# Feed-forward phase of a fused forward and backward pass: operands turned on TensorE ahead of their group, turned stores in SP's queue, half chunks in pairs

## The chip, the core and the metric

The kernel runs on one core of a Trainium2 chip. Its time is device microseconds, the median of a few runs. The core has a matrix engine (PE, with PEld for its weight loads), three engines for elementwise work (DVE, ACT, POOL) and SP, which here only issues DMAs. POOL issues DMAs too. The two issuers have a queue each, and 16 DMA engines serve both.

## The reference

A transformer layer with recurrent memory attention and a gated feed-forward network (FFN), and the gradients of all its inputs, in bf16:

```
h  = x + A(layernorm(x), mem0, Wq, Wk, Wv, Wo)    # segments of 32 rows, one after the other
h2 = h + (silu(hn @ w_gate) * (hn @ w_up)) @ w_down, hn = layernorm(h)
_out, _vjp = jax.vjp(_f, A_x, A_mem0, A_Wq, A_Wk, A_Wv, A_Wo, B_w_gate, B_w_up, B_w_down)
_grads = _vjp(grad_out)
```

x has 2048 rows of 448, the FFN is 1792 wide, and the attention has 16 heads of 256 and 8 rows of memory. The memory that leaves one segment enters the next, so attention runs through 64 segments in order, and its backward pass through the same 64 in reverse.

## The kernel before

Four stages follow each other on PE. `forward_chain` runs the 64 segments. `ffn_phase` does the FFN forward and backward for 8 **groups** of 256 rows (G = 2 tiles of 128). `backward_chain` runs the 64 segments backward; it is a Python generator, and its first loads are written into the program from within the FFN's last group by calls of `back()`, one step up to each `yield`. `tail_phase` forms the weight gradients from what the other stages stored to DRAM.

The order on each engine comes from a scheduler at build time: it takes ready instructions by priority, which falls with their place in the program. `tc.issue_after(ins)` puts an instruction behind another one on its engine. On the chip each engine, and SP's and POOL's queue of DMAs, then works strictly in that order: an instruction that waits holds all behind it.

SBUF is cut by hand. `W`, `A` and `B` are three arenas (arW, arA, arB in the profile), and `A(35, ...)` is a view that starts at KB 35 of each partition. Buffers of different stages lie over each other, so many waits are for a place to become free.

One group (lines 874 to 971; n counts the groups in order, gi is the group's place in the rows):

- `load_in` (L279) fetches the rows of h and of grad_out through SP. DVE normalises h into `hn` (L887). Both are 448 wide and padded to 512, so that they make KC = 4 chunks of 128 columns; the fourth is half zeros, and so are the weights' last 64 rows (memsets at L826 to L832).
- hn and grad_out are turned into `hnT` and `doT`: groups 0 and 1 by PE (L893) with a copy out of PSUM by DVE or ACT (L894), groups 2 to 7 by DMA transposes in SP's queue (L896).
- `proj` (L856) multiplies weights by a turned operand: 7 PSUM banks, in each 2 column blocks by 4 chunks, 56 matmuls of 128x256 (L862). It runs three times: gate (ACT sigmoid L904, DVE product L905), up (ACT copy L908, DVE product z L909), and dz from `doT` (ACT copy L912). PSUM has 5 banks for this.
- DVE forms the derivative of silu in three passes of 128x3584 (L914, L921, L922), and from it and dz the gradients u and g (L941 to L943).
- PE multiplies z by w_down (28 matmuls, L934), and u and g by the turned weights (56 matmuls, L958). `ln_bwd` (L252 to L263) ends the tile on DVE.
- `tmajor` (L850) turns z, u and g with DMA transposes in SP's queue (L853) into three staging buffers in turn, and POOL stores those (L854). The last group is turned by PE (`tmajor_pe`).

Around the phase: the forward pass leaves four blocks of 512 KB whose turned copies go out through two staging buffers in arA (transposes L554 in SP's queue, stores L511 `X_o` in POOL's). Group 1 writes its gate into the same places. At the other end the steps of `back()` load, in this order: q, k and three quarters of Wk turned (L1044); Wo turned (L1046); Wv turned (L1050); `vT`, the values of the last segment (L1011), which lies over the last group's dz; and, behind the FFN, the first quarter of Wk (L1054) and Wq (L1055).

Of the kernel before, what the change touches and what calls it, by code (L numbers as in the profile page):

```python
# [15 lines left out]
P = 128  # L16
# [249 lines left out]
class _FFNLoads:  # L266
# [19 lines left out]
    def rows(self, dst, src):  # L286
        k, sync = self.k, self.k.nc.sync
        sync.dma_start(out=dst[:, 0:3, :], in_=src[0:3 * P, :].rearrange("(kc p) n -> p kc n", p=P))
        return sync.dma_start(out=dst[0:64, 3, :], in_=src[3 * P:k.D, :])

    def turned_rows(self, dst, src):
        sync = self.k.nc.sync
        sync.dma_start(out=dst[:, 0:3, :], in_=src[:, 0:3, :])
        return sync.dma_start(out=dst[0:64, 3, :], in_=src[0:64, 3, :])
# [17 lines left out]
class _TailLoads:  # L312

    def __init__(self, k):
        W, A, NT, NB = k.W, k.A, k.NT, k.NB
        self.k = k
        self.first = [W(17.5 + 4 * i, 2048) for i in range(3)] + [A(4 * i, 2048) for i in range(4)]
        self.slots = [A(48 + 4 * i, 2048) for i in range(3)] + [W(60, 2048), W(92, 2048)] + [W(96 + 4 * i, 2048) for i in range(7)] \
            + [W(32 + 4 * i, 2048) for i in range(7)] + [W(64 + 4 * i, 2048) for i in range(7)] + [A(17.5 + 4 * i, 2048) for i in range(4)] + self.first[0:3]
# [474 lines left out]
def ffn_phase(k: _K, back):  # L794
# [24 lines left out]
    dz_b = [W(54.5, G, FC, P), A(49, G, FC, P)]  # L819
    tstg_b = [W(92, FC, P), W(120.5, FC, P), B(5, FC, P)]  # L820
# [4 lines left out]
    for i in range(4):  # L825
        nc.gpsimd.memset(hn_b[i][:, D:DP], 0.0)  # L826
        nc.gpsimd.memset(dout_b[i][:, D:DP], 0.0)
    for i in range(2):
        nc.gpsimd.memset(dhb_b[i][:, D:DP], 0.0)
    nc.gpsimd.memset(Wg_sb[64:P, 3, :], 0.0)  # L830
    nc.gpsimd.memset(Wu_sb[64:P, 3, :], 0.0)
    nc.gpsimd.memset(WdT_sb[64:P, 3, :], 0.0)  # L832

# [15 lines left out]

    def tmajor(src, t, tt, dst):  # L850
        stg = tstg_b[rot[0] % 3]
        rot[0] += 1
        nc.sync.dma_start_transpose(out=stg, in_=src[:, tt].rearrange("p f n -> p (f n)"))  # L853
        nc.gpsimd.dma_start(out=dst[t * P:(t + 1) * P, :], in_=stg.rearrange("p f n -> p (f n)"))  # L854

    def proj(Wt, xT, fn):  # L856
        for fp in range(FC // 2):
            ps = k.ps1()
            for f2 in range(2):
                c = 2 * fp + f2  # L860
                for kc in range(KC):
                    nc.tensor.matmul(ps[:, f2 * 256:(f2 + 1) * 256], lhsT=Wt[:, kc, c * P:(c + 1) * P], rhs=xT[:, kc, :],  # L862
                                     start=(kc == 0), stop=(kc == KC - 1))
            fn(ps[:].rearrange("p (f t n) -> p t f n", f=2, t=G), slice(2 * fp, 2 * fp + 2))
# [9 lines left out]
    for n, gi in enumerate(list(range(last - 1)) + [last, last - 1]):  # L874
        hnT, doT = hnT_b[n % 2], doT_b[n % 2] if n < last else doT_last
        t1 = t1_b[n == last]
        if n > 1:
            load_in(n, gi)
        if n == last - 3:
            rstd(NT - 4, NT)  # L880
        for tt in range(G):
            t = G * gi + tt
            i = 2 * (n % 2) + tt
            rows = slice(t * P, (t + 1) * P)
            h_t, hn_t, dout_t = h_b[i], hn_b[i], dout_b[i]
            with tc.issue_after(k.last_x["v"].ins):
                nc.vector.tensor_scalar(out=hn_t[:, 0:D], in0=h_t, scalar1=mv2[:, t, 0:1], scalar2=rstd2[:, t:t + 1],  # L887
                                        op0=ALU.subtract, op1=ALU.mult)
            for src, dst in ((hn_t, hnT), (dout_t, doT)):
                if n < 2:  # L890
                    pt = k.ps1()[:].bitcast(BF16)
                    for kc in range(KC):
                        nc.tensor.transpose(pt[:, kc * P:(kc + 1) * P], src[:, kc * P:(kc + 1) * P], k.ident[:, :])  # L893
                    k.evac(dst[:, :, tt * P:(tt + 1) * P], pt[:, 0:DP].rearrange("p (c n) -> p c n", n=P))  # L894
                else:
                    nc.sync.dma_start_transpose(out=dst[:, :, tt * P:(tt + 1) * P], in_=src)  # L896
            nc.gpsimd.dma_start(out=dr["HN"][rows, :], in_=hn_t[:, 0:D])
        if n == last:
            back()
        e = n % 2  # L900
        g, z, dz, u, sg = g_b[e], z_b[e], dz_b[e], u_b[e], sg_b[e]
# [12 lines left out]
        to_v = nc.vector.tensor_tensor(out=t1, in0=g, in1=sg, op=ALU.mult)  # L914
# [6 lines left out]
        nc.vector.tensor_tensor(out=t1, in0=g, in1=t1, op=ALU.subtract)  # L921
        nc.vector.tensor_tensor(out=sg, in0=t1, in1=sg, op=ALU.add)  # L922
        proj(Wu_sb, hnT, up)
# [16 lines left out]
        for tt in range(G):  # L940
            nc.vector.tensor_tensor(out=u[:, tt], in0=dz[:, tt], in1=u[:, tt], op=ALU.mult)  # L941
            nc.vector.tensor_tensor(out=u[:, tt], in0=u[:, tt], in1=sg[:, tt], op=ALU.mult)
            nc.vector.tensor_tensor(out=g[:, tt], in0=dz[:, tt], in1=g[:, tt], op=ALU.mult)  # L943
        if n == last:
            back()
            for tt in range(G):
                tmajor_pe(z, G * gi + tt, tt, dr["Zt"], (W(120.5, F), B(5, F))[tt])
        for tt in range(G):
# [13 lines left out]
            ln_bwd(k, [(dh_t, dout_b[2 * e + tt][:, 0:D], 0, D)], pdh[:, 0:D], hn_b[2 * e + tt][:, 0:D], rstd2[:, t:t + 1], t1f[:], junk)  # L962
# [3 lines left out]
            nc.gpsimd.dma_start(out=dr["DHb"][rows, :], in_=dh_b)  # L966
        if n == last:
            for tt in range(G):
                t = G * gi + tt
                tmajor_pe(u, t, tt, dr["DGP"], A(7 * tt, F))  # L970
                tmajor_pe(g, t, tt, dr["DU"], A(7 * tt + 3.5, F))


def backward_chain(k: _K):
# [16 lines left out]
    vT = A(48, 16, 2 * L)  # L991
# [4 lines left out]
    dh_h = [B(9.875, 448).bitcast(FP32), A(50.5, 448).bitcast(FP32)]  # L996
# [452 lines left out]
```

## Time and profile before

| | us |
|---|---|
| median of 5 runs | 3155.65 (3151.09 to 3157.26) |
| the profiled execution: its time | 3155.65 |
| the profiled execution: its span, first to last instruction | 3153.8 |
| forward segments, up to the first matmul of L862 | 1060.8 |
| FFN, from there to the first L1093 of the backward pass | 332.4 |
| backward segments, from there to the first L1329 of the tail | 1091.8 |
| tail | 668.7 |

The profiled execution took as long as the median run, and 1.85 us lie outside its span. The stages are read from PE's timeline by the line numbers. Over the whole span PE is busy for 92%, DVE for 43%, ACT for 34% and POOL for 21%.

The timeline prints start, duration, engine, line, operation, output<-inputs and the count of merged instructions; in brackets the engine's idle time before and what ended it. The waits view prints who waited for whom, with us in total, times, and the longest.

### The profile page before, as it was taken

Reading aid. Unit: us, or ns where it says so; the run is one execution under the profiler, and the core shown is the slowest. Engines: PE = TensorE matmul, PEld = TensorE weight load, DVE = VectorE, ACT = ScalarE, POOL = GpSimd, SP = SyncE. Lnnn points to the kernel's source line nnn. Section 1 sums busy time; section 2 is a strip of 40 time slices with the busy share of each in tenths; the row PEclk is TensorE's granted clock in tenths of the full one; section 3 lists DMA queues with packets and bytes.
Section 4 is the critical chain, followed back from the end, with each engine's and each line's share of the span. In section 5 each row is a group of like instructions: output and inputs, shape, how many; then the busy total and the mean of one; then the engine's idle time right before and its main releaser. Section 6 shows DMA issues by size and latency. Waiting matters only on the chain. (4 is left out here: it accounts for less than half of the span.)

```text
span 3153.8 us, 108004 instructions
## 1 busy us (share of the span) xinstructions
PE 2911.4 (92%) x47486; PEld 1759.2 (56%) x47486; DVE 1370.2 (43%) x3437; ACT 1060.4 (34%) x2505; POOL 667.1 (21%) x1540
## 2 busy tenths in 40 slices
PE   5999999999988869979999999999999799999998
PEld 3555555455544556656666666666666454444443
DVE  4555555455555567764445444454444201111110
ACT  2444444344444323333344333343334101111210
POOL 2222222222222221121112111121211111211111
PEclk9999999999999989999999999999999999999999
DMA  6667766766755998894545545546544899969941
GB/s 238 166 176 173 175 170 169 179 165 168 194 162 165 260 224 196 204 322 116 139 133 145 135 132 140 133 130 153 136 134 137 259 283 248 198 179 188 200 148 64
DMA packets 758075, 554.79 MB, mean 176 GB/s; under 512 B 621924, under 2 KB 656596, under 8 KB 755172
## 3 DMA queue, kind: packets, MB, share of 16 engines
q1 hardware_dynamic: 702436, 372.51, 49.8%
q0 software_dynamic: 55168, 175.36, 16.5%
q8 instruction: 373, 6.11, 0.8%
q14 instruction: 98, 0.80, 0.1%
HBM read 167.32 MB, written 234.23 MB: 127 GB/s over the span
## 5 line engine op out<-in xcount | busy, mean ns | idle before, releaser
L75 DVE CAST arA<-psf 128x256 bf16<-128x256 f32 (+3 forms) x933 | 426.9, 480 | 788.3 <-PE psf L1308 258.9
L76 ACT CAST arA<-psf 128x96 bf16<-128x96 f32 (+5 forms) x915 | 352.4, 409 | 1047.3 <-PE psf L1308 256.5
L1142 PE MATMUL po<-arW,arA 128*32 128x448 bf16 x6144 | 348.3, 357 | 6.7 <-DMA arW<-Tk 6.7
L1308 PE MATMUL psf<-arW,arA 128*128 128x512 bf16 x960 | 241.9, 379 | 0.0
L1093 PEld LDWEIGHTS <-arW 128*128 128x128 bf16 x8192 | 213.4, 96 | 28.2 <-issue 28.1
L1308 PEld LDWEIGHTS <-arA 128*128 128x128 bf16 x1440 | 136.0, 98 | 165.1 <-issue 13.7
L1093 PE MATMUL psf<-arA,arW 128*128 128x40 bf16 x8192 | 217.2, 180 | 8.8 <-DVE arA L1168 5.1
L644 PE MATMUL psf<-arW,arA 128*64 128x512 bf16 x1536 | 220.3, 388 | 0.0
L1142 PEld LDWEIGHTS <-arA 128*32 128x32 bf16 x6144 | 152.9, 97 | 118.3 <-issue 9.6
L533 PE MATMUL psf<-arW,arA 128*32 128x512 bf16 x3072 | 193.6, 385 | 12.5 <-DVE arA L731 12.5
L862 PE MATMUL psf<-arW 128*128 128x256 bf16 x1288 | 149.9, 277 | 42.2 <-DVE arA L905 13.1
L862 PEld LDWEIGHTS <-arW 128*128 128x128 bf16 x1344 | 133.3, 99 | 68.1 <-issue 36.6
L76 ACT CAST arB<-psf 128x64 bf16<-128x64 f32 (+3 forms) x384 | 121.8, 318 | 146.2 <-PE psf L537 109.7
L689 PE MATMUL po<-arW,arA 128*32 128x256 bf16 (+1 forms) x4096 | 142.9, 265 | 10.5 <-DVE arA L75 7.5
L1103 ACT COPY arA<-psf 128x1024 bf16<-128x1024 bf16 x128 | 123.3, 1015 | 2.1 <-PE psf L1102 0.6
L1070 PEld LDWEIGHTS <-arW 128*128 128x128 bf16 x2048 | 86.4, 99 | 62.9 <-issue 59.2
L533 PEld LDWEIGHTS <-arA 128*32 128x32 bf16 x3072 | 70.5, 96 | 90.1 <-DVE arA L731 18.1
L462 PE MATMUL fx<-arA,arW 128*128 128x64 bf16 (+1 forms) x2048 | 84.2, 195 | 33.1 <-ACT arB L76 19.3
L689 PEld LDWEIGHTS <-arA 128*32 128x32 bf16 x4096 | 94.8, 97 | 32.7 <-DVE arA L75 10.5
L76 ACT COPY arA<-psf 128x512 bf16<-128x512 bf16 (+2 forms) x136 | 79.0, 582 | 99.6 <-DVE arA L75 91.1
L1070 PE MATMUL psf<-arB,arW 128*128 128x80 bf16 x2048 | 96.6, 201 | 14.8 <-DVE arB L1123 5.2
L462 PEld LDWEIGHTS <-arW 128*128 128x128 bf16 (+1 forms) x2048 | 70.7, 98 | 55.5 <-issue 32.7
(288 smaller groups left out, 4607.7 us busy)
## 6 DMA issues: line engine op xcount, KB each, us to landing
arW<-T SPq DMA_DIRECT2D x256, 128.0 KB
X_o<-arA SPq DMA_DIRECT2D x33, 512.0 KB
T<-arA SPq DMA_DIRECT2D x64, 256.0 KB
X_v<-arA POOLq DMA_DIRECT2D x32, 512.0 KB, 6.0
X_k<-arA POOLq DMA_DIRECT2D x32, 512.0 KB, 3.8
X_q<-arA POOLq DMA_DIRECT2D x32, 512.0 KB, 3.2
out_dram<-arA POOLq DMA_DIRECT2D x90, 128.0 KB, 4.0
VG<-arA SPq DMA_DIRECT2D x64, 160.0 KB
```

The lines of the kernel that those rows point to most:

```text
L75: return nc.vector.tensor_copy(out=out, in_=in_)
L76: return nc.scalar.copy(out=out, in_=in_)
L462: nc.tensor.matmul(banks[w][:, i * 64:(i + 1) * 64], lhsT=lhsT, rhs=xr[lo:hi, kc, :], start=(kc == 0 and i == 0), stop=(kc == KC - 1), ski ...
L533: nc.tensor.matmul(banks[w][32 * q:32 * q + 32, :], lhsT=hT_roll[:, kc, sl, M:L], rhs=(Wq_sb, Wk_sb)[w][:, kc, col(q, b)], start=(kc == 0) ...
L644: nc.tensor.matmul(pV[b][64 * g:64 * g + 64, 0:512], lhsT=hT_flat[:, kc, sl * L:sl * L + 64], rhs=Wv_sb[:, kc, n * 512:(n + 1) * 512], sta ...
L689: nc.tensor.matmul(pO[32 * q:32 * q + 32, 0:w], lhsT=xblk[:, j, r * SEG:(r + 1) * SEG], rhs=Wo_sb[:, cj(j), 256 * dh:256 * dh + w], start= ...
L862: nc.tensor.matmul(ps[:, f2 * 256:(f2 + 1) * 256], lhsT=Wt[:, kc, c * P:(c + 1) * P], rhs=xT[:, kc, :], start=(kc == 0), stop=(kc == KC - 1))
L1070: nc.tensor.matmul(ps[b][:, i * 2 * L:(i + 1) * 2 * L], lhsT=lhs[:, at, :], rhs=rhs_bd[:, cl // 2, :, :].rearrange("p g n -> p (g n)"), st ...
L1093: nc.tensor.matmul(pss[b][:, jj * L:(jj + 1) * L], lhsT=WoT_sb[:, kc, c * P:(c + 1) * P], rhs=do_roll[:, kc, sl, :], start=(kc == 0), stop ...
L1103: nc.scalar.copy(out=dO_sb[:, 8 * hf:8 * hf + 8, :], in_=ph.rearrange("p (c n) -> p c n", n=P))
L1142: nc.tensor.matmul(pH[32 * (j % 4):32 * (j % 4) + 32, 0:D], lhsT=blk[nm][:, j, r * SEG:(r + 1) * SEG], rhs=WT[:, cj(j), :], start=(nm == " ...
L1308: nc.tensor.matmul(pa[2 * kc + g][:, 0:w], lhsT=lhs_of(b)[:, kc * P:(kc + 1) * P], rhs=rhs_of(b, g), start=(b == 0), stop=(b == nblk - 1), ...
```

## The change

- **Half chunks paired.** The fourth chunk of `proj` is multiplied over 64 rows instead of 128, so nothing has to be zeroed there. Two banks are worked on together. Their first three chunks come one bank after the other, then the four half chunks alternate between partitions 0 to 63 and 64 to 127. For that both operands hold the last 64 rows twice: the weight loads `rows` and `turned_rows` fetch them twice (three more DMAs of 224 KB), the norm gets a second pass of 64 columns, and POOL copies 64 columns of grad_out. The seventh bank has no partner.
- **Turned by PE.** All groups are turned by PE, copied out by ACT alone. The norm of group n + 1 is pinned behind the last product of group n on DVE (`normed`), and the transposes are written between the two tiles' gradient products (`turned`). The loads of a group are issued one group earlier.
- **Turned stores in SP's queue.** `tmajor` issues the store of the staging buffer before, after its own transpose.
- **Silu's derivative.** 1 - sigmoid is now made by POOL, and DVE makes two passes of 128x3584 instead of three, written behind the up projection.
- **The last group and the backward pass.** hn and grad_out of the last group are copied by POOL (`kept`), and its dz moves to A(7). `vT` moves to A(49.5), is loaded in the first step of `back()`, and that step loads Wk from block 2 on instead of from 8; the first two blocks come with Wv. The call of `back()` that loaded `vT` is gone.
- **Buffers.** The backward pass's five blocks rotate by one more, and the first buffers of the tail's ring move with them; 11 blocks instead of 12 are fetched ahead of its end.

```diff
     def rows(self, dst, src):
...
-        return sync.dma_start(out=dst[0:64, 3, :], in_=src[3 * P:k.D, :])
+        for w in (0, 64):
+            sync.dma_start(out=dst[w:w + 64, 3, :], in_=src[3 * P:k.D, :])
...
-        self.first = [W(17.5 + 4 * i, 2048) for i in range(3)] + [A(4 * i, 2048) for i in range(4)]
+        self.first = [W(17.5 + 4 * i, 2048) for i in range(3)] + [A(8 + 4 * i, 2048) for i in range(4)]
...
+    dz_last = A(7, G, FC, P)
+    kept = [[A(2 + i, D) for i in range(2)], [A(4 + i, D) for i in range(2)]]
...
-    for i in range(4):
-        nc.gpsimd.memset(hn_b[i][:, D:DP], 0.0)
-        nc.gpsimd.memset(dout_b[i][:, D:DP], 0.0)
...
-    nc.gpsimd.memset(Wg_sb[64:P, 3, :], 0.0)
...
         nc.sync.dma_start_transpose(out=stg, in_=src[:, tt].rearrange("p f n -> p (f n)"))
-        nc.gpsimd.dma_start(out=dst[t * P:(t + 1) * P, :], in_=stg.rearrange("p f n -> p (f n)"))
+        saved()
+        unsaved.append((dst[t * P:(t + 1) * P, :], stg.rearrange("p f n -> p (f n)")))
...
-        for fp in range(FC // 2):
-            ps = k.ps1()
+        for f0 in range(0, FC // 2, 2):
+            fps = range(f0, min(FC // 2, f0 + 2))
+            ps = {fp: k.ps1() for fp in fps}
...
+            for fp in fps:
+                for f2 in range(2):
+                    for kc in range(KC - 1):
+                        mm(fp, f2, kc, 0, P)
             for f2 in range(2):
...
+                for fp in fps:
+                    w = 64 * (fp - f0)
+                    mm(fp, f2, KC - 1, w, w + 64)
...
+    def normed(n, after):
+        for tt in range(G):
+            t = G * turns[n] + tt
+            i = 2 * (n % 2) + tt
+            for o, c0 in ((0, 0), (D, D - 64)):
+                w = D if o == 0 else 64
+                with tc.issue_after(after.ins):
+                    nc.vector.tensor_scalar(out=hn_b[i][:, o:o + w], in0=h_b[i][:, c0:c0 + w], scalar1=mv2[:, t, 0:1],
+                                            scalar2=rstd2[:, t:t + 1], op0=ALU.subtract, op1=ALU.mult)
+            nc.gpsimd.tensor_copy(out=dout_b[i][:, D:DP], in_=dout_b[i][:, D - 64:D])
+            nc.gpsimd.dma_start(out=dr["HN"][t * P:(t + 1) * P, :], in_=hn_b[i][:, 0:D])
+
+    def turned(n):
...
+                    nc.tensor.transpose(pt[:, kc * P:(kc + 1) * P], src[:, kc * P:(kc + 1) * P], k.ident[:, :])
+                k.evac(dst[:, :, tt * P:(tt + 1) * P], pt[:, 0:DP].rearrange("p (c n) -> p c n", n=P), "s")
...
-        if n > 1:
-            load_in(n, gi)
+        if 0 < n < last:
+            load_in(n + 1, turns[n + 1])
...
-                else:
-                    nc.sync.dma_start_transpose(out=dst[:, :, tt * P:(tt + 1) * P], in_=src)
...
         proj(Wg_sb, hnT, gate)
-        to_v = nc.vector.tensor_tensor(out=t1, in0=g, in1=sg, op=ALU.mult)
+        nc.gpsimd.tensor_scalar(out=t1, in0=sg, scalar1=-1.0, scalar2=1.0, op0=ALU.mult, op1=ALU.add)
+        proj(Wu_sb, hnT, up)
+        to_v = nc.vector.tensor_tensor(out=t1, in0=g, in1=t1, op=ALU.mult)
...
-        nc.vector.tensor_tensor(out=t1, in0=g, in1=t1, op=ALU.subtract)
         nc.vector.tensor_tensor(out=sg, in0=t1, in1=sg, op=ALU.add)
-        proj(Wu_sb, hnT, up)
...
-            nc.vector.tensor_tensor(out=g[:, tt], in0=dz[:, tt], in1=g[:, tt], op=ALU.mult)
+            to_v = nc.vector.tensor_tensor(out=g[:, tt], in0=dz[:, tt], in1=g[:, tt], op=ALU.mult)
         if n == last:
-            back()
...
+        else:
+            saved()
+            normed(n + 1, to_v)
...
+            if tt == 0 and n < last:
+                turned(n + 1)
...
-    vT = A(48, 16, 2 * L)
+    vT = A(49.5, 16, 2 * L)
...
     load_seg(NSEG - 1)
-    nc.sync.dma_start(out=WkT_sb[:, 8:MC], in_=dr["Tk"][:, 8:MC])
+    load_v(NSEG - 1)
+    nc.sync.dma_start(out=WkT_sb[:, 2:MC], in_=dr["Tk"][:, 2:MC])
...
     nc.sync.dma_start(out=WvT_sb, in_=dr["Tv"])
+    nc.sync.dma_start(out=WkT_sb[:, 0:2], in_=dr["Tk"][:, 0:2])
     yield
-    load_v(NSEG - 1)
-    yield
-    nc.sync.dma_start(out=WkT_sb[:, 0:8], in_=dr["Tk"][:, 0:8])
...
-        blk = {nm: blk_b[(3 * tb + i + 2) % 5] for i, nm in enumerate("vkq")}
+        blk = {nm: blk_b[(3 * tb + i + 3) % 5] for i, nm in enumerate("vkq")}
```

## The prediction

> **What bounds the kernel now.** I read the page first. PE is busy for 92% of the span and DVE for 43%, but the shares mix four stages, and the change touches the third of them in time, the FFN, and the two seams around it. So I went on to PE's timeline of the FFN and its seams, to the waits of the same windows, and to busy times by group.
>
> At the first seam PE stands still twice, with 6.5 us of work between:
>
> ```profile
> 1098.11 0.72 PE L893 MATMUL psf<-ident,arW 128*128 128x128 bf16 x10
> 1108.02 6.54 PE L862 MATMUL psf<-arW 128*128 128x256 bf16 x40 [9.18 <-DVE lnb_m2s L259]
> 1127.68 9.54 PE L862 MATMUL psf<-arW 128*128 128x256 bf16 x64 [13.12 <-DVE arA L905]
> ...
> ACT arA L904 <- DMA X_o<-arA: 18.8, 1, 18.8
> DVE arA L905 <- DMA X_o<-arA: 16.6, 1, 16.6
> ```
>
> The first gap is group 1's norm, queued on DVE behind ln_bwd. The second is the 6th PSUM bank: DVE and ACT may not write the gate of group 1 until the last `X_o` store has left arA. That store was issued at 1123.45 and landed at 1126.85. Its transpose L554 was issued at 1117.66 by SP, behind the transposes of group 0. The clock: PE was granted 0.50 to 0.59 in the slices with the gaps, 1.00 around them.
>
> In the steady part, from the first L958 of group 1 to that of group 7, a group takes 35.7 to 39.3 us:
>
> ```profile
> 1192.24:1231.57 39.33, 34.95 (x257) 24.93 (x255) 31.64 (x47) 14.58 (x24) 8.03 (x15) 1.00 0.89 207
> 1343.57:1379.24 35.67, 35.47 (x277) 25.69 (x275) 27.05 (x42) 13.87 (x24) 14.29 (x18) 1.00 0.93 258
> ...
> PE psf L862 <- DMA arW<-arW: 8.5, 4, 4.1
> PE psf L862 <- DVE arA L909: 6.1, 9, 2.6
> ```
>
> Columns are us; then PE, PEld, DVE, ACT and POOL busy, clock, DMA share and GB/s. The reader is to see that PE bounds this part, with DVE close behind (31.6 of 39.3), and that PE's named waits are few: 8.5 us for operands that the DMA turns, 6.1 us for DVE to free a bank, over six groups and 225.5 us.
>
> At the second seam the first backward segment lasts from 1393.26 to 1426.06, 32.8 us, where the next takes 15.7:
>
> ```profile
> 1403.57 1.05 PE L1111 MATMUL psf<-arA 128*64 128x40 bf16 x32 [5.99 <-DMA arA<-VG]
> 1418.82 5.12 PE L1142 MATMUL po<-arW,arA 128*32 128x448 bf16 x64 [6.66 <-DMA arW<-Tk]
> 1426.06 3.35 PE L1093 MATMUL psf<-arA,arW 128*128 128x40 bf16 x128 [0.28 <-DVE arA L1168]
> ...
> 1419.41 0.53 POOL L1060 MEMSET omb<- 128x512 f32 x1 [13.32 <-DMA DH<-dh_t]
> ```
>
> PE waits for vT and for the first quarter of Wk. The last line matters as much: the buffer `omb`, into which this segment's result goes, is cleared only at 1419.41, when POOL has seen DH land.
>
> **First seam, group 0 and the gate of group 1.** The early norm and transposes remove the 9.18 us gap, and pairing and the smaller DVE load may shorten group 0. None of it counts: group 1 fills five banks and waits for `X_o` in any case, now from earlier. So the term is the shift of the `X_o` landing. DMA share is 1.0 to 1.2 in all slices from 1050 to 1130. The change adds 3 x 224 KB of weights ahead: 0.67 MB at the 250 to 350 GB/s of these slices is 2 to 3 us. Three stores of z and u come into SP's queue ahead of the last L554, at 0.4 to 1.0 us of issue each (the rows of L283 here) and at no wait if the transpose before has landed. Against it: fewer stores share POOL's queue with X_o, and a scheduler that puts L554 ahead of one transpose of 448 KB gives back 5.75 us (the row of L853 at 1111.85). Bounds -6 and +8; I take **+2**, the bytes alone. The removed memsets (1.6 us each) are on POOL at 1041 to 1050, beside the last segment: nothing.
>
> **Group 1 behind X_o.** From 1127.68 to 1153.71 PE loses 3.3 us to L909, behind DVE's passes of 2.0 us (L914 to L922). One of three goes, the others move behind the up projection, where only ACT copies banks. I let two thirds go: **-2**.
>
> **Six steady groups.** The waits for turned operands go: **-8.5**. With them the one cold stretch: L958 of group 3 behind the 4.09 us wait takes 12.44 instead of 10.76: **-1.7**. Of the 6.1 us of DVE waits two thirds go: **-4**. The price is PE's: 16 transposes a group at 0.056 us (x10 in 0.72 with 0.22 of one's own length): 0.9, six times **+5.4**. Their copies are on ACT, four of 0.59 (L76, 128x512), beside the second tile's 28 matmuls (5.3 us): hidden. The norm behind the last product is ready in time by the rows: dz to the last L943 6.5 us, norm 0.8, extra passes 0.3 to 0.8 (bounds L257 0.15 and L887 0.39 each); PE needs it 10.6 us behind dz (28 of L934 and 28 of L958 at 0.189). If the loads are not there, it isn't; see the rival.
>
> Pairing. A full chunk takes 0.109 us (56 in 6.27). Half chunks over 64 rows and 128 columns stand in the trace in L462:
>
> ```profile
> 866.27 0.49 PE L462 MATMUL fx<-arA,arW 128*128 128x64 bf16 x11
> ...
> 866.27 0.74 PE L462 MATMUL fx<-arA,arW 128*128 128x64 bf16 x16
> 866.95 0.40 PE L533 MATMUL psf<-arW,arA 128*32 128x512 bf16 x4
> ```
>
> Eleven full ones give 0.030 a step; the sixteen, of which the last four are halves, take 0.68 to the next instruction instead of 0.48. So going to 64 rows and back costs 0.20. Four halves in two rounds then cost 0.22 + 0.20 = 0.42 against 0.44 for four full chunks: nothing won. The seventh bank has two halves alone: +0.20. A projection gains or loses: all switches free, 6 x 0.109 = -0.65; halves one after another, 4 x 0.20 = +0.8; I take +0.2, since the four half-row matmuls of L652 (64*64, 512 wide) all start within 0.01 us. Three a group, six groups: **+3.6** (-12 to +14).
>
> The Trainium skill bears on this. TensorEngine Tiling, Key Properties, says that changing the tiling mode drains the engine, and TensorE: Matmul & The Clock Gate, Part 3, that matmuls on different row groups start about 4 ns apart. The halves of L462 started 0.03 us apart, as full ones do, so the row doesn't show the second rule for 128 columns. By the second rule without the first the six groups would win 12 us, by the row they lose 14.
>
> POOL's 1 - sigmoid: by MEMSET (128x2048, 1.82) it takes 3.2 us for 3584, by the copy of 128x128 (0.30) up to 8. The up projection gives it 6 us and dz another 6 before DVE needs its product: nothing. POOL's copy L1181 took 1.01 instead of 0.22 beside DVE products, so the two disturb each other. SBUF — State Buffer, section "SBUF: two separate sides", says that a GpSimd operation and a VectorE one with two SBUF inputs exclude each other for a whole instruction. By that DVE could stand up to 3.2 us in a group; in the up projection DVE's products read PSUM, so I count none.
>
> POOL loses its waits for transposes (38 us for Zt alone here), which nobody waited for.
>
> Sum of the six groups: -8.5 - 1.7 - 4 + 5.4 + 3.6 = **-5.2**.
>
> **Second seam.** The surplus of the first segment is 32.8 - 15.7 = 17.1 us. vT and nearly all of Wk are there early. What is late next? Wv: issued at 1387.9, when the FFN's output has left its place, 3.6 MB at 400 GB/s, so there at 1397; needed at 1399.6 (the next segment uses it 6.3 us in). Wq: SP could issue it only at 1398.18, behind vT's 9.66 us; now behind Wv, there at about 1407, needed at 1405. Then `omb`: POOL stores DH at 1405.0, behind the DHb store that landed at 1402.6; it landed 14 us later beside 4.5 MB of Wq and Wk. With Wq done at 1407 I expect 1412 to 1416. L1160 ran at 1424.06; it could run at 1414.5: **-9.5**. Bounds: -6 if DH lands only 3 us sooner and with a queue behind, -14 if it costs nothing.
>
> **Tail.** PE waited 13.2 us before the tail for a load of `M_v`, which POOL issued at 2475.0 when the last store of X_q had landed (2474.4). The rotated blocks put that place under a block of X_k, whose store landed at 2471.0: **-2** (0 to -3.4). One fetched block less: 0, as 11 blocks give PE 12.5 us (1.14 each) to load the next.
>
> **Sum.** +2 - 2 - 5.2 - 9.5 - 2 = -16.7, from the profiled execution, which is also the median: 3155.65 - 16.7 = **3139**.
>
> **Rivals.**
> - *Halves don't overlap.* For: L462. Against: L652, at other columns. 0.6 more a projection, 1.8 a group, 6.6 groups that PE bounds: +12, 3151.
> - *The seams give all.* X_o lands 6 us sooner instead of 2 later, and DH doesn't hold the first segment: -8 - 4.5, 3126.5. For: both are queues that the change makes shorter. Against: DMA share over 1.0 in both.
> - *SP's queue makes every group late: slower.* Each of six stores a group waits in SP's queue until its transpose has landed; POOL bore such waits, 131 us for 32 stores in these six groups, 4.1 each. Behind them stand the loads of the next group, behind these the norm on DVE and the transposes in the middle of PE's products: PE stands there. At 4 us a group, with the cold clock of 1.7, 6 x 5.7 = +34: 3173. It decides the sign of the whole from 2.8 us a group (17 / 6). For: the queue is strict. Against: the next transpose is issued before the wait, four of ten transposes a group are gone, and the loads have some 25 us.
> - That pairing does nothing is inside the first two.
>
> **How the numbers follow.** Forecast 0.50 (3128 to 3149 by its bounds), halves in series 0.18, seams 0.17, SP's queue 0.15. Measurement tells 0.2% from no change, 6.3 us: faster is under 3149.3, slower over 3162. Faster: 0.46 of the forecast, 0.06, 0.17: 0.69. Same: 0.04 + 0.12 + 0.02 = 0.18. Slower 0.13. The range leaves out SP's queue and the end of the seams' case: 3122 to 3158.
>
> **What would show it.** Right: no wait of L862 for arW; X_o still ends the long gap, near 1129; groups of 36 to 37 us; the first backward segment at 22 to 24 us, ended by `omb`; L1287 about 2 us sooner behind the last segment. Wrong: halves more than 0.03 apart; PE waiting for DVE or loads at the transposes; a first segment under 19 or over 28; X_o shifted by over 8.

## The result, and the profile after

| | us | runs |
|---|---|---|
| before, median | 3154.59 (3140.82 to 3172.72) | 63 |
| after, median | 3154.76 (3142.75 to 3164.79) | 37 |
| ratio after / before | 0.9997, 95% interval 0.9989 to 1.0005 | |
| profiled execution after: span | 3155.3 (before 3153.8) | 1 |

No change that can be measured, where 3139 was forecast. All of the change is in the trace, though, and it moved the time in three places, in different directions. In the changed kernel the three projections of `proj` are L868, the transposes by PE L909, the products with w_down and with the turned weights L963 and L989. On POOL, L900 is the copy that pads grad_out and L943 is 1 - sigmoid. On DVE, L934, L938 and L945 are the gate product, the up product and the product with 1 - sigmoid.

**First seam.** PE's timeline, columns as before:

```profile
1106.63 4.62 PE L868 MATMUL psf<-arW 128*128 128x256 bf16 x40
1130.46 18.18 PE L868 MATMUL psf<-arW 128*128 128x256 bf16 x128 [19.21 <-DVE arA L934]
1153.89 2.43 PE L989 MATMUL fx<-arW,arA 128*128 128x448 bf16 x12
```

The two gaps have become one. It ends 75.6 us after the last output product of the forward pass (75.1 before). The first product of L989 in group 1 comes at 1153.89, where the old one came at 1153.71, in a run whose forward pass ended 2.3 us later. The last `X_o` was issued at 1123.99 and landed 5.2 us later, near 1129 as forecast, and DVE began the gate at 1129.72. (For DVE's wait the profile names DH, a store issued at 1124.77; it landed only after that start, at 1129.95.)

**The groups.** PE by group (us; PE, PEld, DVE, ACT, POOL busy; clock, DMA share, GB/s), and the waits of the same stretch:

```profile
1153.89:1197.54 43.65, 38.50 (x270) 22.93 (x269) 27.93 (x51) 16.10 (x29) 11.23 (x17) 0.92 0.71 180
...
1276.20:1313.92 37.72, 35.74 (x269) 21.87 (x268) 27.42 (x46) 14.63 (x27) 7.98 (x11) 1.00 0.76 188
1313.92:1356.21 42.29, 37.11 (x270) 22.41 (x269) 27.43 (x46) 14.63 (x27) 8.04 (x12) 0.96 0.78 180
```

```profile
POOL arW L900 <- DMA arW<-in_grad_out_dram: 47.0, 5, 11.3
...
PE psf L868 <- DVE arA L938: 17.9, 6, 5.2
DVE arW L945 <- POOL arW L943: 17.3, 5, 5.1
```

The waits for operands turned by DMA are gone, as forecast. In their place PE waits 17.9 us for DVE to free banks, DVE waits 17.3 us for POOL, and POOL 47.0 us for loads. The six groups take 239.9 us instead of 225.5. The timelines of POOL, DVE and PE in the worst group show the chain:

```profile
1334.08 0.24 POOL L900 COPY arW<-arW 128x64 bf16<-128x64 bf16 x1 [9.79 <-DMA arW<-in_grad_out_dram]
...
1337.16 0.24 POOL L900 COPY arW<-arW 128x64 bf16<-128x64 bf16 x1 [1.50 <-PE psf L868]
1337.36 3.17 POOL L943 TENSOR_SCALAR arW<-arA 128x3584 bf16<-128x3584 bf16 x1
...
1334.16 1.29 DVE L938 TENSOR_TENSOR arA<-psf,arA 128x512 bf16<-128x512 f32 x2 [0.93 <-ACT arA L937]
1340.57 2.03 DVE L945 TENSOR_TENSOR arW<-arA,arW 128x3584 bf16<-128x3584 bf16 x1 [5.12 <-POOL arW L943]
1342.51 3.08 DVE L938 TENSOR_TENSOR arA<-psf,arA 128x512 bf16<-128x512 f32 x5
...
1343.25 3.04 PE L868 MATMUL psf<-arW 128*128 128x256 bf16 x14 [5.18 <-DVE arA L938]
```

Read it from the top. POOL's queue holds the pad copies of the *next* group in front of this group's 1 - sigmoid, and they wait for the next group's grad_out. The last sigmoid of this group ended at 1332.40, so L943 starts 4.96 us later than it could. (The profile puts the second copy's wait down to PE; SP issued its load of grad_out only at 1331.45, so it may be the load again.) DVE's queue holds L945, which needs L943, in front of five of the seven up products. So banks are not freed, and PE stands for 5.18 us. In the six groups L943 starts 4.93, 2.52, 2.31, 1.75, 4.96 and 0.09 us after the last sigmoid, and PE's gaps are 5.15, 2.74, 2.54, 1.98, 5.18 and 0.30. Behind three of them (5.15, 2.54 and 5.18) the dz projection takes 7.7 to 9.1 us instead of 6.4, and those groups have a clock of 0.92 to 0.96; behind the one of 2.74 it takes 6.4, at 1.00.

**Second seam.** PE's and POOL's timelines:

```profile
1407.84 3.53 PE L1125 MATMUL psf<-arA,arW 128*128 128x40 bf16 x128 [0.25 <-DVE arA L75]
...
1424.96 2.43 PE L1174 MATMUL po<-arW,arA 128*32 128x448 bf16 x24 [4.28 <-DMA arW<-Tq]
1429.26 1.92 PE L1196 MATMUL psf<-sel,omb 128*128 128x32 f32 x8 [0.56 <-DVE omb L1192]
1431.46 4.21 PE L1125 MATMUL psf<-arA,arW 128*128 128x40 bf16 x128 [0.28 <-DVE arA L1200]
...
1428.14 0.52 POOL L1092 MEMSET omb<- 128x512 f32 x1 [10.65 <-DMA DH<-dh_t]
```

The first backward segment takes 23.6 us instead of 32.8. `omb` is cleared 20.3 us into it instead of 26.2. The load of Wq is as late: PE waits 4.28 us for it. From the first backward matmul to the end the profiled execution takes 1747.4 us instead of 1760.5. Of these 13.1 us, 9.2 are the first segment's. Another 4.5 lie between the starts of the second and the last segment (1016.2 instead of 1020.7); a second execution of the kernel before took 1017.1 there, so they may be run to run.

So of 3155.3 - 3153.8 = +1.5, the forward pass gives +2.3 (the same code, run to run), the first seam -2.2, the groups +14.4, the rest -13.1.

### The profile page after: what moved, and what is told of

Same layout as the page of the kernel before. It is cut to its first block, busy times and chain, and to the rows that moved or that the text cites. A ratio compares the mean times of both kernels' runs of the same rounds, so it can differ in the third digit from the quotient of the medians.

```text
span 3155.3 us, 108184 instructions
## 1 busy us (share of the span) xinstructions
PE 2920.6 (93%) x47582; PEld 1736.5 (55%) x47582; DVE 1360.4 (43%) x3441; ACT 1068.9 (34%) x2533; POOL 672.6 (21%) x1515
## 4 chain that ended last, share of the span: by engine, by line
PE 74%; issue 8%; DVE 7%; DMA 5%; ACT 3%; POOL 2%; SPq 0%; ACTq 0%; POOLq 0%; DVEq 0%
PE psf L1340 8%; PE po L1174 7%; PE psf L1125 7%; PE psf L535 5%; PE psf L646 5%; PE po L691 4%; PE psf L1102 4%; PE psf L1361 4%; PE psf L868 3%; PE fx L1238 3%; PE fx L989 2%; PE fx L464 2%; DVE arA L75 2%; PE fx L1345 2%; PE psf L1196 2%
## 5 line engine op out<-in xcount | busy, mean ns | idle before, releaser
L1125 PEld LDWEIGHTS <-arW 128*128 128x128 bf16 x8192 | 213.3, 96 | 27.2 <-issue 27.0
L868 PE MATMUL psf<-arW 128*128 128x256 bf16 (+1 forms) x1288 | 156.0, 284 | 38.3 <-DVE arA L934 19.2
L868 PEld LDWEIGHTS <-arW 128*128 128x128 bf16 (+1 forms) x1344 | 106.2, 99 | 94.6 <-issue 80.5
L1102 PEld LDWEIGHTS <-arW 128*128 128x128 bf16 x2048 | 86.4, 99 | 62.6 <-issue 57.2
L464 PE MATMUL fx<-arA,arW 128*128 128x64 bf16 (+1 forms) x2048 | 85.0, 196 | 32.8 <-ACT arB L76 19.4
L76 ACT COPY arA<-psf 128x512 bf16<-128x512 bf16 (+2 forms) x138 | 80.3, 582 | 94.8 <-DVE arA L75 92.6
L1102 PE MATMUL psf<-arB,arW 128*128 128x80 bf16 x2048 | 96.8, 201 | 14.4 <-DVE arB L1155 5.1
L464 PEld LDWEIGHTS <-arW 128*128 128x128 bf16 (+1 forms) x2048 | 71.3, 99 | 55.4 <-issue 32.9
```

Source lines behind the costliest of these rows:

```text
L76: return nc.scalar.copy(out=out, in_=in_)
L464: nc.tensor.matmul(banks[w][:, i * 64:(i + 1) * 64], lhsT=lhsT, rhs=xr[lo:hi, kc, :], start=(kc == 0 and i == 0), stop=(kc == KC - 1), ski ...
L868: nc.tensor.matmul(ps[fp][:, f2 * 256:(f2 + 1) * 256], lhsT=Wt[lo:hi, kc, c * P:(c + 1) * P], rhs=xT[lo:hi, kc, :], start=(kc == 0 and f2 ...
L1102: nc.tensor.matmul(ps[b][:, i * 2 * L:(i + 1) * 2 * L], lhsT=lhs[:, at, :], rhs=rhs_bd[:, cl // 2, :, :].rearrange("p g n -> p (g n)"), st ...
L1125: nc.tensor.matmul(pss[b][:, jj * L:(jj + 1) * L], lhsT=WoT_sb[:, kc, c * P:(c + 1) * P], rhs=do_roll[:, kc, sl, :], start=(kc == 0), stop ...
```

## The experiments

The theory: the gain at the second seam is real, and POOL's in-order queue eats it in the groups, since a small copy that waits for a load stands ahead of 1 - sigmoid. Rivals: the loads are late for everyone, so a cure at POOL only moves the wait; POOL's 1 - sigmoid slows DVE by a shared port; pairing or the stores in SP's queue cost the time.

All stages below are read from PE's timeline of each profiled execution, in us. "Seam" is from the forward pass's last output product to the first product with the turned weights in group 1, in brackets the end of the long gap. "Steady" is the length of a group in which PE waits neither for a DMA nor behind a late POOL, "first segment" the first backward one.

| kernel | ratio to before (95%) | seam | six groups | steady | first segment |
|---|---|---|---|---|---|
| before, two executions | 1 | 101.2 (75.1), 98.6 (72.8) | 225.5, 226.6 | 36.2 | 32.8, 35.3 |
| after | 0.9997 (0.9989 to 1.0005) | 99.0 (75.6) | 239.9 | none | 23.6 |
| e1 pad copies behind | 0.9931 (0.9914 to 0.9948) | 97.5 (75.0) | 218.3 | 36.06 | 23.6 |
| e2 product behind | 0.9928 (0.9911 to 0.9945) | 101.5 (80.0) | 216.0 | 35.69 | 25.1 |
| e3 derivative on DVE | 0.9996 (0.998 to 1.0011) | 105.7 (78.6) | 231.7 | 37.80 | 23.9 |
| e4 start alone, and e11 | 0.9979 (0.9965 to 0.9994) | 98.9 (73.6), 102.3 (75.5) | 233.7, 227.2 | none | 26.0, 26.0 |
| e5 both pins | 0.9929 (0.9909 to 0.9948) | 101.9 (80.3) | 216.0 | 35.69 | 23.7 |
| e6 e5 unpaired | 0.9897 (0.9882 to 0.9912) | 93.0 (70.8) | 212.3 | 35.12 | 23.8 |
| e7 e5, stores in POOL's queue | 0.996 (0.9943 to 0.9977) | 101.3 (79.8) | 216.0 | 35.69 | 26.5 |
| e8 e5, P loaded later | 0.9936 (0.991 to 0.9961) | 98.1 (75.9) | 216.0 | 35.69 | 24.1 |
| e9 pairing undone | 0.9879 (0.9863 to 0.9896) | 91.5 (70.5) | 213.1 | 35.12 | 25.4 |
| e10 e9, weights loaded twice | 0.9897 (0.9883 to 0.9912) | 101.3 (80.6) | 213.1 | 35.12 | 23.6 |
| e13 e10, P loaded later | 0.9901 (0.9881 to 0.9922) | 96.8 (74.8) | 213.1 | 35.12 | 24.8 |

**e1, the copies behind 1 - sigmoid.**

```diff
-            nc.gpsimd.tensor_copy(out=dout_b[i][:, D:DP], in_=dout_b[i][:, D - 64:D])
+            with tc.issue_after(one_less.ins) if n > 0 else nullcontext():
+                nc.gpsimd.tensor_copy(out=dout_b[i][:, D:DP], in_=dout_b[i][:, D - 64:D])
...
-        nc.gpsimd.tensor_scalar(out=t1, in0=sg, scalar1=-1.0, scalar2=1.0, op0=ALU.mult, op1=ALU.add)
+        one_less = nc.gpsimd.tensor_scalar(out=t1, in0=sg, scalar1=-1.0, scalar2=1.0, op0=ALU.mult, op1=ALU.add)
```

> One edit to the changed kernel: the GpSimd copies that pad the next group's gradient rows (L900) are put behind this group's 1 - sigmoid (L943) in GpSimd's queue; no other engine's order changes. My theory: in the changed kernel L943 starts 4.93, 2.52, 2.31, 1.75, 4.96 and 0.09 us after the last sigmoid of its group in the six steady groups, because L900 stands in front of it and waits for late loads; DVE's product L945 waits for L943 with five up products behind it, and TensorE stands 5.15, 2.74, 2.54, 1.98, 5.18 and 0.30 us for its banks. Expected: L943 starts within 0.1 us of the last sigmoid, the six gaps shrink by what L943 gains to about 0.2 to 0.3 us each, 16 us less, and the slow clock behind them (about 5 us) goes too: 3134 us, ratio to before 0.993. Rival, late loads: the copies only move, the next group's turns then wait for the same loads: about 3150. Rival, shared port: L943 itself slows VectorE: 3152 or more.

3132.84 us, -0.69%. POOL's, DVE's and PE's timelines of the same place in the same group (in e1's lines L946 is 1 - sigmoid, L903 the copy, L948 the product), and PE's only wait in the six groups:

```profile
1314.38 3.17 POOL L946 TENSOR_SCALAR arW<-arA 128x3584 bf16<-128x3584 bf16 x1 [1.55 <-ACT arA L936]
1317.51 2.21 POOL L903 COPY arW<-arW 128x64 bf16<-128x64 bf16 x2
...
1317.59 2.03 DVE L948 TENSOR_TENSOR arW<-arA,arW 128x3584 bf16<-128x3584 bf16 x1 [0.25 <-POOL arW L946]
...
1320.28 6.36 PE L868 MATMUL psf<-arW 128*128 128x256 bf16 x56 [0.31 <-DVE arA L941]
```

```profile
PE psf L868 <- DVE arA L941: 1.9, 6, 0.4
```

POOL now waits for the sigmoid and not for the load, DVE waits 0.25 us for POOL, PE 0.31 for DVE. The theory's number came out (3134 expected). "The loads are late for everyone" falls: PE waits for them nowhere, and POOL itself only 2.5 us in the six groups. So does the shared port as the cause: 1 - sigmoid still runs on POOL, for the same 3.17 us, and the time is gone.

**e2, the product behind the up products.**

```diff
-        to_v = nc.vector.tensor_tensor(out=t1, in0=g, in1=t1, op=ALU.mult)
+        with tc.issue_after(k.last_up.ins):
+            to_v = nc.vector.tensor_tensor(out=t1, in0=g, in1=t1, op=ALU.mult)
```

`k.last_up` is the seventh up product.

> One edit to the changed kernel: DVE's product t1 = g * (1 - sigmoid) (L945) is put behind the last of the seven up products (L938) of its group; GpSimd keeps its order and its late L943. My theory (GpSimd's late result blocks DVE's queue, and so the banks): the TensorE waits of 18.4 us for DVE L938 vanish and the slow clock behind them too: 3131 to 3134 us, ratio 0.993. Rival, late loads: the loads hold the group elsewhere, at the turns by TensorE: about 3150. Rival, VectorE is short of time: its two full-size operations (2.02 us each) now lie behind the up products, the products with the gradient come 4 us later and TensorE waits there, 6 x 2 us: about 3145.

3134.30 us, -0.72%. POOL's copies still wait 43.1 us (47.0 in the changed kernel); PE waits for nothing in the six groups, and the group is 0.37 us shorter than in e1:

```profile
POOL arW L900 <- DMA arW<-in_grad_out_dram: 43.1, 5, 10.5
```

So the late POOL cost nothing once DVE had no bank to free behind its wait, and VectorE was not short of time.

**e3, the derivative on VectorE again.**

```diff
-        nc.gpsimd.tensor_scalar(out=t1, in0=sg, scalar1=-1.0, scalar2=1.0, op0=ALU.mult, op1=ALU.add)
-        proj(Wu_sb, hnT, up)
-        to_v = nc.vector.tensor_tensor(out=t1, in0=g, in1=t1, op=ALU.mult)
+        to_v = nc.vector.tensor_tensor(out=t1, in0=g, in1=sg, op=ALU.mult)
...
+        nc.vector.tensor_tensor(out=t1, in0=g, in1=t1, op=ALU.subtract)
         nc.vector.tensor_tensor(out=sg, in0=t1, in1=sg, op=ALU.add)
+        proj(Wu_sb, hnT, up)
```

> One edit to the changed kernel: the three operations of the gate's derivative are all on VectorE again, ahead of the up products, as in the kernel before; GpSimd has no part in it. My theory: the waits for GpSimd go, and the two waits of the kernel before for DVE come back (6.1 us in eight groups, of which I had claimed 4): 3138 us, ratio 0.995. If GpSimd's own work slows VectorE by a shared port, this is clearly better than putting the copies or the product behind (by 3 us and more); by my theory it is 3 to 5 us worse than those. Rival, late loads: about 3150.

3152.20 us: a miss, 14 us above what I expected. One steady group of it, and of e5, e6 and e9:

```profile
1280.12:1317.92 37.80, 36.28 (x269) 21.69 (x269) 29.26 (x46) 14.63 (x27) 5.85 (x10) 1.00 0.79 190
```

```profile
1260.27:1295.97 35.70, 35.70 (x270) 21.81 (x269) 27.61 (x46) 14.63 (x27) 7.90 (x11) 1.00 0.84 201
```

```profile
1247.46:1282.59 35.13, 35.13 (x270) 25.54 (x269) 27.85 (x45) 15.34 (x27) 7.90 (x12) 1.00 0.82 205
```

```profile
1249.34:1284.46 35.12, 35.12 (x269) 25.56 (x268) 26.93 (x43) 15.37 (x27) 7.55 (x10) 1.00 0.84 204
```

In e5, e6 and e9 PE is busy for the whole group at full clock; in e3 it isn't, at 37.80 us. So the derivative on DVE costs 37.80 - 35.69 = 2.11 us a group, where I had counted 4 us in all six. Its seam is longer too, 105.7 us: from the end of the gap on it takes 27.0, where e2 and e5 take some 21.5; the rest stays open. Seam and six groups together take 337.4 us here and 338.9 in the changed kernel, so 1 - sigmoid behind a waiting copy cost about as much as the derivative on DVE.

**e4, the start of the backward pass alone**, put into the kernel before: the hunks of `kept`, `dz_last`, the tail's buffers and `backward_chain`, nothing else.

```diff
-    vT = A(48, 16, 2 * L)
+    vT = A(49.5, 16, 2 * L)
...
-    nc.sync.dma_start(out=WkT_sb[:, 8:MC], in_=dr["Tk"][:, 8:MC])
+    load_v(NSEG - 1)
+    nc.sync.dma_start(out=WkT_sb[:, 2:MC], in_=dr["Tk"][:, 2:MC])
```

> One part of the change alone, put into the kernel before: the loads and buffers for the start of the backward pass (values and first weights loaded earlier, the last group's rows copied aside, its gradient tile and the output stages moved). The FFN groups keep their transposes by DMA, their order and the unpaired projections. My theory: the first backward segment falls from 32.8 us to some 24 and the tail starts 2 us earlier, the steady groups stay at 225.5 us from the first to the seventh: 3143.5 us, ratio 0.9965. Rival: the gain comes from the turns by TensorE, which free the sync queue for these loads; then alone it gives less than 3 us: 3152.

3148.50 us, -0.21%, at the weak end of what I expected. The first segment falls to 26.0 us, and from the first backward matmul to the end it takes 1747.1 (before 1760.5). Its groups were 8.2 us longer in that execution. Another profile of this kernel and one of the kernel before tell what that is worth:

> The kernel before with the backward start alone, a second look, for the profile: in the first look its backward pass and tail gained 13.5 us and its groups lost 8.2 us (233.7 us from the first to the seventh against 225.5), though their code is that of the kernel before. If the loss is that run's own, the groups take 225 to 228 us now; if the part itself slows the groups, 232 to 235.

> The kernel before, a second look, for the profile: how far do the groups' 225.5 us and the first backward segment's 31.2 us stand for the kernel? If DMA landings vary from run to run, the groups differ by 3 us and more; otherwise by less than 1 us.

227.2 and 226.6 us: by that forecast the longer groups were that run's own. In it PE waited 11.2 us for operands turned by DMA, where the kernel before waited 8.5, and the granted clock was 0.93 to 0.97 in five of the six groups. The kernel before differs from itself by 1.0 us in the groups and by 2.5 in the first segment (35.3; what the expectation calls 31.2 is 32.8 in the trace). From the first backward matmul to the end it was 1751.0 against 1761.1. The part alone gives 10 to 13 us in the trace; the times (-2 to -11 us) agree with the lower end.

**e5, both pins.**

> Both pins together: pad copies behind 1 - sigmoid and the product t1 behind the up products. Each alone has brought 0.993. My theory: they cure one stall, so together they bring hardly more than one: groups of 35.7 us as with the product behind, ratio 0.9925, within 0.1% of either alone. Rival, two separate costs: the gains add, ratio 0.987.

3130.82 us, 0.9929: no more than either alone. One stall with two cures.

**e6, both pins and unpaired projections.** `proj` as in the kernel before, the 64 weight rows loaded once, their upper rows zeroed.

```diff
-        for f0 in range(0, FC // 2, 2):
...
+        for fp in range(FC // 2):
+            ps = k.ps1()
...
+                for kc in range(KC):
+                    nc.tensor.matmul(ps[:, f2 * 256:(f2 + 1) * 256], lhsT=Wt[:, kc, c * P:(c + 1) * P], rhs=xT[:, kc, :],
+                                     start=(kc == 0), stop=(kc == KC - 1))
...
+    for Wt in (Wg_sb, Wu_sb, WdT_sb):
+        nc.gpsimd.memset(Wt[64:P, 3, :], 0.0)
```

> Both pins, and the projections unpaired as in the kernel before: full 128-row matmuls, a bank at a time, the weights' upper rows of the last chunk zero. My prediction's term: pairing costs 3.6 us, so this is 3.6 us faster than both pins with pairing. From the changed kernel's trace (a pair's matmuls take 0.53 us with their transitions against five full ones' 0.545): pairing is worth nothing, within 2 us. Rival, the halves save time: this is 8 us and more slower (36 pairs of full matmuls at 0.109 us more in six groups would be some 8 us).

3119.36 us, 0.9897, some 10 us faster than e5. My later reading ("worth nothing") was wrong and the prediction's term right: 35.69 - 35.12 = 0.57 us a group, 3.4 in six. The other part is at the seam, 93.0 instead of 101.9; there the weight rows are loaded once and POOL's order differs too (see e10 and e13).

**e7, the turned stores in POOL's queue again.**

```diff
-        saved()
-        unsaved.append((dst[t * P:(t + 1) * P, :], stg.rearrange("p f n -> p (f n)")))
+        nc.gpsimd.dma_start(out=dst[t * P:(t + 1) * P, :], in_=stg.rearrange("p f n -> p (f n)"))
```

> Both pins, and the stores of the turned products back in GpSimd's queue, as in the kernel before. My theory: the stores wait there for their turns and hold GpSimd's 1 - sigmoid again; DVE now has the up products ahead of its own wait, so TensorE feels only what is over about 5 us: 0 to 6 us slower than both pins, 3135. Rival, the sync queue with the stores makes the loads late and so the groups long: 3 us or more faster than both pins.

3139.34 us, 0.996. The profiled execution doesn't show a loss: POOL waits over 100 us for turns, the groups are 216.0 as in e5, the span is 3132.4 against 3134.0. It was one of the fastest of twelve, and where the 0.3% of the times lie stays open. That the stores in SP's queue hurt is not seen. But both kernels have the pins: whether in the changed kernel it was those stores that made the loads of grad_out late, so that POOL's copies waited, no run tells.

**e8, the load of P behind the last memory-row copy.** At the forward pass's end the changed kernel's POOL has the load of P (which waits for its own store) ahead of a copy that PE needs: 5.07 us of wait on PE.

```diff
-        nc.gpsimd.dma_start(out=P_sb.rearrange("p h n -> p (h n)"), in_=dr["P_all"][s])
+        with tc.issue_after(k.last_mb.ins) if s == NSEG - 1 else nullcontext():
+            nc.gpsimd.dma_start(out=P_sb.rearrange("p h n -> p (h n)"), in_=dr["P_all"][s])
```

> Both pins, and the load of P for the backward pass is put behind the last memory-row copy in GpSimd's queue at the end of the forward pass, as the kernel before has it. The changed kernel's trace shows TensorE 5.1 us at that copy (the last memory output product), and the first gate product 8.6 us later than before. My theory: this wait costs nothing, since group 1 waits 16 to 22 us for the forward's last stores anyway: first gate product 5 us earlier, long gap of group 1 as much longer, time unchanged within 2 us. Rival: the stores hang on that copy too, and the whole moves up: 5 us faster than both pins.

3131.03 us, 0.9936: within the intervals the same as e5. In the trace the gap ended 4.4 us sooner after the forward pass (75.9 instead of 80.3), which speaks for the rival and against my theory; the times don't show it; its forward pass, the same code, took 9.6 us longer than in e5, so its span says nothing.

**e9, pairing undone in the changed kernel**, without any pin: unpaired `proj`, weight rows loaded once, pads and upper rows zeroed once by memsets, no pad copies, no 64-column norms. To e6's edit of `proj` and the loads comes:

```diff
-            for o, c0 in ((0, 0), (D, D - 64)):
...
+            with tc.issue_after(after.ins):
+                nc.vector.tensor_scalar(out=hn_b[i][:, 0:D], in0=h_b[i], scalar1=mv2[:, t, 0:1],
+                                        scalar2=rstd2[:, t:t + 1], op0=ALU.subtract, op1=ALU.mult)
-            nc.gpsimd.tensor_copy(out=dout_b[i][:, D:DP], in_=dout_b[i][:, D - 64:D])
...
+    for i in range(4):
+        nc.gpsimd.memset(hn_b[i][:, D:DP], 0.0)
+        nc.gpsimd.memset(dout_b[i][:, D:DP], 0.0)
```

> One part of the change undone, the pairing with all that it brought: full 128-row matmuls, zeros set once in the pads and in the weights' upper rows, hence no pad copies in GpSimd's queue, no 64-column norms on VectorE, no second load of 64 weight rows. Nothing is pinned. My theory: what ate the gain of the change is this part. The gaps of 17.9 us behind GpSimd and some 5 us of slow clock go, the projections give 3.7 us (35.12 against 35.69 us a group, as the unpaired kernel with both pins shows), and group 1 comes some 6 us sooner after the forward pass: 3124 us, ratio 0.990. Rival: the copies are not what holds 1 - sigmoid, only one of several: 3140 or more. Rival: the product t1 ahead of the up products still costs, 2 us a group: 3135.

3120.71 us, 0.9879: faster than both kernels, with the lowest ratio of this study (e6's interval overlaps it). 1 - sigmoid needs no pin, since nothing that waits for a load stands before it. Steady groups take 35.12 us, and PE waits for DVE 0.6 us in all six, so the rival of 2 us a group falls.

**e10 and e13, where the seam's part lies.** e10 is e9 with the 64 weight rows loaded twice and no zeros among them (the pads of the operands are zero); in it POOL's order at the end of the forward pass is that of the changed kernel. e13 mends that order by the edit of e8.

> As the kernel with the pairing undone, but the 64 weight rows of the last chunk are still loaded twice (0.69 MB more at the end of the forward pass) and the pads alone hold zeros. My theory: the groups are the same (35.1 us), but the forward's last stores share the DMA engines with the extra load, at 266 GB/s 2.6 us, and the first group after them comes 3 to 6 us later: ratio 0.9915. Rival: the load is hidden: same time as the kernel with the pairing undone, within 1.5 us.

> As the kernel without pairing but with the weight rows loaded twice, and with the load of P put behind the last memory-row copy in GpSimd's queue, the order that the kernel with the pairing undone has. Between those two the long gap of group 1 ended 80.6 and 70.5 us after the last output product of the forward pass. If the queue's order makes the difference, the gap ends at 70 to 72 us and the ratio is 0.988; if the second load makes it, at 79 to 81 and 0.9897; my theory: each has half, 75 to 76 us, ratio 0.989.

0.9897 and 0.9901. PE's waits at the long gap, in e9, e10 and e13:

```profile
PE psf L870 <- DVE arA L924: 21.5, 1, 21.5
```

```profile
PE psf L870 <- DVE arA L924: 25.2, 1, 25.2
```

```profile
PE psf L870 <- DVE arA L924: 21.7, 1, 21.7
```

The gap ends 70.5, 80.6 and 74.8 us after the forward pass: by these, 5.8 us for the queue's order and 4.3 for the second load of 0.69 MB, in one profile each. The other profiles of kernels whose groups are all turned by PE say how far that holds: with neither cost it ends at 70.5 and 70.8 (e9, e6), with the load alone at 74.8 and 75.9 (e13, e8), with both anywhere from 75.0 to 80.6 (the changed kernel, e1, e2, e3, e5, e7, e10). So the load, with the memsets that it replaces, stands out by some 4 us, and the order by anything from nothing to 6; what decides that stays open. The times can't tell e10 from e13.

## Why the prediction was wrong

| step | forecast | measured |
|---|---|---|
| first seam and group 1 behind it | +2 - 2 = 0 | the gap's end +0.4 (75.6; before 75.1 and 72.8), group 1 behind it 23.4 instead of 26.0 and 25.8: -2.2 in all, within the spread of the seam in the kernel before (101.2, 98.6) |
| DMA waits and cold clock gone | -8.5 - 1.7 | gone; before's groups are 8.6 and 9.6 over six of 36.16 |
| transposes by PE | +5.4 | 0.90 a group from the first one's start to the next product's: +5.4 |
| pairing | +3.6 | 0.57 a group: +3.4 (e6 against e5) |
| DVE's waits | -4 | 1.94 a group: -11.6 (before against e6) |
| POOL's 1 - sigmoid | 0 | 239.9 - 216.0 = +23.9 (after against e2 and e5) |
| second seam | -9.5 | 32.8 (35.3 in the second execution) to 23.6: -9.2 |
| tail | -2 | L1319 came 2 us sooner behind the last segment (L1287 before), but the first L1361 followed it after 3.4 us, where L1329 had followed after 0.8; no gain seen |

The step that failed is "The up projection gives it 6 us and dz another 6 before DVE needs its product: nothing." Its duration was right, 3.17 us for 3.2. Two queues were not looked at. In front of it, on POOL, stand the pad copies, which the prediction had named among small extra passes and not as instructions that wait for a load. Behind the one that needs it, on DVE, stand five up products with PSUM banks in hand. When DVE needs the *result* is not the question; what DVE may not do while it waits is. By e1 and e2, either order alone brings it back: 21.6 and 23.9 us of the groups.

The DVE term was mis-sized as well, in the other direction. The transposes take this much of PE in a group of the changed kernel, 1160.08 - 1159.18 = 0.90 us (1.06 with the last one's own length):

```profile
1159.18 1.06 PE L909 MATMUL psf<-ident,arW 128*128 128x128 bf16 x16
1160.08 5.46 PE L989 MATMUL fx<-arW,arA 128*128 128x448 bf16 x28
```

e6's steady group, in which PE is never idle, has them and takes 35.12 us. A steady group of the kernel before has none and takes 36.16, so DVE costs it 36.16 - (35.12 - 0.90) = 1.94 us; e3, with the halves paired, gives 2.11. The prediction took 4 us from the 6.1 of named waits over six groups. In that sum the waits for turned operands hide those for DVE: three groups with 1.7 to 4.1 us of the first have 0.2 to 0.3 of the second, and the one group of 36.16 us has 1.72, in three waits:

```profile
1291.06 1.03 PE L862 MATMUL psf<-arW 128*128 128x256 bf16 x8 [0.23 <-DVE arA L909]
...
1293.60 1.03 PE L862 MATMUL psf<-arW 128*128 128x256 bf16 x8 [0.74 <-DVE arA L909]
...
1296.13 6.27 PE L862 MATMUL psf<-arW 128*128 128x256 bf16 x56 [0.74 <-DVE arA L909]
```

With this term right and the hold at nothing, the steps lead from 225.5 - 8.6 + 5.4 + 3.4 - 11.6 to 214.1, six groups of 35.69 us (213.0 with e3's figure). e2 and e5 have 216.0, since their second and last groups take 36.01 and 37.26. That the measured 3154.76 lies inside the stated 3122 to 3158 is luck: the range left out late loads behind a strict queue, and a DVE term 7.6 us better than counted took a part of the 23.9 off.

"SP's queue makes every group late" was near in kind: a strict queue, late loads, a cold clock behind the gaps. It named the wrong place. The loads did have time before the turns: in the worst group the second copy was done at 1337.40, and the turns came at 1361.50. The first copy had stood in POOL's queue, waiting for its load, since 1324.29. "Halves don't overlap" fell: the halves of a pair start 0.004 us apart in the trace (1303.726 and 1303.730). But the step to 64 rows takes 0.205 us and the step back 0.20, where full ones follow at 0.109, so a full one and four halves take 0.53 us against 0.545 for five full ones, and the seventh bank pays its switches alone.

On the rules that the prediction weighed: the Trainium skill, TensorEngine Tiling (Array Packing), Key Properties, says that a change of mode drains the engine, and TensorE: Matmul & The Clock Gate, Part 3, that matmuls on different row groups start some 4 ns apart. The 0.1 us at each switch and the 0.004 us agree with both.

What is argued and not shown: that the slow clock behind the gaps follows from them. In e1 and e2 both are gone (1.00 in all six groups), but in the changed kernel a gap of 2.54 us has it and one of 2.74 hasn't. One reading of the clock in the prediction was off, and nothing was counted from it: in the slices next to those of 0.50 and 0.59 it was 0.84 and 0.87, not 1.00.

## What to carry to other kernels

Before work is given to an idle engine, read two queues: what stands ahead of the new instruction there and waits for something slower, and what stands behind the instruction that will wait for its result. A small helper (here a copy of 64 columns) that waits for a load belongs behind whatever the critical engine needs; better, make it unnecessary. A trick that saves no time on its own engine can still cost through what feeds it: pairing's copies, where the change had put them in POOL's queue, cost 22 to 24 us, and its second load some 4, against 3.4 for its matmuls.

## What the runs showed of the hardware

- Beside a DVE product with two SBUF operands, POOL's copy of 64 columns took 2.03 us instead of 0.23. In e1 three groups show it: the copy of 1317.69 to 1319.72 beside L948 at 1317.59 to 1319.62, and 1281.62 to 1283.66 and 1245.57 to 1247.59 alike. Beside up products, which read PSUM, 1 - sigmoid kept its 3.17 us and DVE's products their 0.68. The Trainium skill, SBUF — State Buffer, section "SBUF: two separate sides", has it so: with two SBUF inputs on DVE the two exclude each other for a whole instruction.
- With the DMA engines full at the first seam (share 1.06 in e9 and 1.08 in e13 from 1040 to 1130 us, 283 GB/s in both), the gap ended 4.3 us later with the second load of the weight rows, in one profile each; 0.69 MB at 283 GB/s would be 2.4.
